# Ninety matmuls of zeros and new planner prices in a gated-linear-attention and expert kernel

## The chip, the core and the metric

The kernel runs on one core of a Trainium2 chip. A core has five engines that run their own queues in order and meet at semaphores: PE (TensorE, the matmuls), DVE (VectorE), ACT (ScalarE), POOL (GpSimd) and SP (SyncE), which here issues all DMA transfers. Matmuls write to PSUM, eight banks; everything else lives in SBUF. DRAM holds inputs and outputs. The metric is device time in microseconds (us), lower is better. The time before is 196.72 us, the median of three runs (196.04 to 197.79).

## The reference

Two steps, one feeding the other. The first is a gated linear attention over 4 batches, 8 heads, 768 positions and a head width of 48; each head keeps a 48 x 48 state that decays per row:

```python
for t in range(S):
    state = alpha[:, :, t, :, None] * state + np.einsum('bhd,bhe->bhde', k[:, :, t], v[:, :, t])
    y[:, :, t] = np.einsum('bhd,bhde->bhe', q[:, :, t], state)
```

The second takes the result as 3072 tokens of width 384 and puts it through a feed-forward layer of 2048 hidden units with a squared ReLU:

```python
h = x @ w_in              # 3072 x 384 @ 384 x 2048
r = np.maximum(h, 0.0)
return (r * r) @ w_out    # 3072 x 2048 @ 2048 x 384
```

All inputs and the output are float32; the kernel multiplies in bfloat16 and sums in float32.

## The kernel before

**Attention.** The 3072 positions are 24 chunks of 128 positions, six to a batch, with all 8 heads of a chunk side by side (384 columns). Within a chunk the recurrence becomes matmuls; from chunk to chunk of a batch only the state goes on. The names used below, with their engine and their line in the profile of before:

- `ln` (ACT, L200): logarithm of alpha. `pm` (PE, L208 and four one-column matmuls L212): running sum of the logarithms, by a triangular matrix `utri`; the last chunk of a batch leaves the one-column matmuls out.
- `ainv`, `am` (ACT, L217, L222): the exponentials of minus and plus that sum. `km` (POOL, L225): k times `ainv`. `qm` (DVE, L228): q times `am`. `vc` (POOL, L204): v cast to `vb`.
- `tr` (PE, L234, eight transposes into the bank `pt`), `qkT` (DVE, L238): both products turned over. From chunk 14 on (`N_PE`) a transposing DMA on SP's queue (L310) does it.
- `sc` (PE, L246): scores. `sm` (DVE, L251): masked scores.
- `av` (PE, L260 and L265, the bank `py`): old state and scores times values; 12 matmuls, or 8 in the first chunk of a batch. `xn` (ACT, L291): result in bfloat16.
- `st` (PE, L274), `dec` (DVE, L282), `sb` (ACT, L286 and L287): state update, decay and a copy.
- `px` (PE, L296), `xT` (DVE, L301): the result turned over, as the feed-forward step needs it; from chunk 14 on by a transposing DMA (L306).

**Feed-forward.** Tokens are taken in nine groups of 2, 2, 3, 3, 3, 3, 3, 3 and 2 chunks. For each group 16 units `ph` (PE, L393, three matmuls each, over 256 or 384 tokens) make the hidden values; `r` (ACT, L398) is the ReLU, `gT` (DVE, L404) its square. Then each chunk of the group has 16 matmuls of 384 columns into `po` (PE, L427; near the end every other chunk uses the bank of `pm`, and the name is `pom`), in four units of four; ACT or DVE empties the bank into `ob` (L441, L443) and SP stores it (L446). Group 0 needs chunks 0 and 1, group 1 needs 2 and 3, group 2 needs 4, 5 and 6.

**Loads.** SP loads four tiles of 192 KB per chunk (`ld_a`, `ld_k`, `ld_q`, `ld_v`, L353), six chunks deep. The eight parts of the two weight matrices (768 KB each, `wst`, L368) stand between chunks: `w_in` after chunk 3, `w_out` after chunk 4; POOL casts each to bfloat16 (L372).

**PSUM.** `ph` has two banks; `po`, `sc`, the transposes' bank and the bank of `pm` and `py` have one buffer each.

**What sets the order.** A planner written in the kernel, `Plan.run`, plays all operations through on its own clock before anything is emitted. Each operation has an engine, a price, a key (a due time; the smallest key among the ready ones goes first), operations it comes after, and a bank it acquires or releases. What the planner starts is emitted in that order, and that is the order on each engine. The planner's clock is no promise: on the chip an engine waits, in order, for what its next instruction needs. A matmul is finished for its users 0.28 us after its price has passed (`HOP`), but PE itself is taken as free once the price has passed. A tile pool gives out its buffers in turn; who takes the buffer anew has to wait until those who used it before are done, and the tile layer puts in the semaphore waits for that.

Of the kernel before, what the change touches and what calls it, by code (L numbers as in the profile page):

```python
# [8 lines left out]
FP32 = mybir.dt.float32  # L9
BF16 = mybir.dt.bfloat16  # L10
# [4 lines left out]
class Plan:  # L15
# [8 lines left out]
        self.cap = dict(capacity)  # L24

    def add(self, eng, cost, key, emit, after=(), behind=(), acquire=None,
            release=None, load=None):
        op = dict(eng=eng, cost=cost, key=(key, len(self.ops)), emit=emit,
                  after=[o for o in after if o is not None],
                  behind=[o for o in behind if o is not None], acquire=acquire,  # L30
                  release=release, load=load, start=None, done=None)
        self.ops.append(op)
        return op

    def run(self):
        ops, cap = self.ops, self.cap
        waiting = {id(o): 0 for o in ops}
        users = {}
        for o in ops:
            uniq = {id(d): d for d in o["after"] + o["behind"]}  # L40
            waiting[id(o)] = len(uniq)
            for d in uniq.values():
                users.setdefault(id(d), []).append(o)
        ready = [(0.0, o) for o in ops if not waiting[id(o)]]
        free = {o["eng"]: 0.0 for o in ops}
        frees = []
        bus = 0.0
        now = 0.0
        order = []
        while len(order) < len(ops):  # L50
            for r in [f for f in frees if f[0] <= now]:
                frees.remove(r)
                cap[r[1]] += 1
            chosen = None
            for t, o in ready:
                if t > now or free[o["eng"]] > now:
                    continue
                if o["acquire"] and cap[o["acquire"]] < 1:
                    continue
                if chosen is None or o["key"] < chosen["key"]:  # L60
                    chosen = o
            if chosen is None:
                later = [max(t, free[o["eng"]]) for t, o in ready] + [f[0] for f in frees]
                now = min(x for x in later if x > now)
                continue
            o = chosen
            ready = [x for x in ready if x[1] is not o]
            o["start"] = now
            free[o["eng"]] = now + o["cost"]
            if o["load"]:  # L70
                bus = max(bus, now + o["cost"]) + o["load"]
                free[o["eng"]] = max(free[o["eng"]], bus - self.QUEUE)
                done = bus + 1.6
            else:
                done = now + o["cost"] + self.HOP.get(o["eng"], 0.1)
            o["done"] = done
            if o["acquire"]:
                cap[o["acquire"]] -= 1
            if o["release"]:
                frees.append((done, o["release"]))  # L80
            order.append(o)
            for u in users.get(id(o), ()):
                waiting[id(u)] -= 1
                if not waiting[id(u)]:
                    ready.append((max([d["done"] for d in u["after"]]
                                      + [d["start"] + d["cost"] for d in u["behind"]]), u))
        self.order = order
        return order
# [3 lines left out]
def kernel(  # L92
# [10 lines left out]
    nc = tc.nc  # L103
    B, H, S, D = q.shape
    HD = H * D
    P = 128
# [6 lines left out]
    DP = 64  # L113
    NS = 4
    NW = 4
    N_PE = 14

    qr = q.rearrange("b h (c p) d -> b c p h d", p=P)
# [26 lines left out]
    groups, n = [], 0  # L145
# [10 lines left out]
    lns = [consts.tile([P, H, DP], BF16, name=f"ln{i}") for i in range(NS)]  # L156
    qks = [consts.tile([P, 2, H, DP], BF16, name=f"qk{i}") for i in range(NS)]
    sbs = [consts.tile([P, NP, 2 * D], BF16, name=f"sb{i}") for i in range(2)]
    xTs = [consts.tile([P, KT, len(cs) * P], BF16, name=f"xT{g}") for g, cs in enumerate(groups)]

    def setup():
        nc.vector.memset(utri, 1.0)
        nc.gpsimd.affine_select(
            out=utri, in_=utri, compare_op=ALU.is_ge, fill=0.0,
            base=0, pattern=[[0, 1], [1, P]], channel_multiplier=-1,
        )
        nc.vector.memset(ones_col, 1.0)
        nc.vector.memset(lns[0], 0.0)
        make_identity(nc, ident)
        for x in lns[1:] + qks[:2]:  # L170
            nc.vector.memset(x, 0.0)
        for x in qks[2:] + sbs:
            nc.gpsimd.memset(x, 0.0)
# [11 lines left out]
    def o(kind, n):  # L185
        return O.get((kind, n))

    def gla(n):
# [119 lines left out]
        def e_qd():  # L308
# [3 lines left out]

        m = n - NW
        add("ln", "ACT", 0.53, e_ln, [o("ld_a", n), o("pm", n - NS)])
        add("vc", "POOL", 0.62, e_vc, [o("ld_v", n), o("av", m), o("st", m)])
        add("pm", "PE", 0.27, e_pm, [o("ln", n), o("av", n - NW + 1)], acquire="m")
        add("ainv", "ACT", 0.49, e_ainv, [o("pm", n), o("km", m)])
        add("am", "ACT", 0.49, e_am,
            [o("pm", n), o("qm", m), o("ainv", n), o("dec", m)], release="m")
        add("km", "POOL", 0.92, e_km, [o("ainv", n), o("ld_k", n), o("st", n - NS), o("tr", n - NS)])  # L320
        add("qm", "DVE", 0.80, e_qm, [o("am", n), o("ld_q", n), o("tr", n - NS)])
        if n < N_PE:
            add("tr", "PE", 0.45, e_tr, [o("km", n), o("qm", n)], acquire="t")
            add("qkT", "DVE", 0.69, e_qkT, [o("tr", n), o("av", m), o("sc", m)], release="t")
# [36 lines left out]
    def load_w(kind, i):  # L361
        n = d_ff // 4 if kind == "wi" else FT // 4
        sl = slice(i * n, (i + 1) * n)
        shape = [P, KT, n] if kind == "wi" else [P, n, d_model]

        def emit():
            x = T[kind, i] = wst.tile(shape, FP32, name="wst", tag="wst")
            nc.sync.dma_start(out=x, in_=w_in_r[:, :, sl] if kind == "wi" else w_out_r[:, sl, :])  # L368

        def cast():  # L370
            dst = w_in_b[:, :, sl] if kind == "wi" else w_out_b[:, sl, :]
            nc.gpsimd.tensor_copy(dst, T[kind, i])  # L372
        ld = plan.add("SP", 0.5, -1e6 + len(loaded), emit,
                      [o("wc", len(weights) - 4)], loaded[-1:], load=2.17)
        loaded.append(ld)
        O["wc", len(weights)] = O["c" + kind, i] = plan.add("POOL", 1.47, -100.0 + len(weights), cast, [ld])
        weights.append(ld)

    group_of = {n: g for g, cs in enumerate(groups) for n in cs}
# [1 line left out]
    def moe(g):  # L381
# [7 lines left out]
        def unit1(f):  # L389
            def e_mm():  # L390
                ph = T["ph", g, f] = ps_h.tile([P, 4 * P], FP32, name="ph")
                for j in range(KT):
                    nc.tensor.matmul(ph[:, 0:tg], lhsT=w_in_b[:, j, f * P:(f + 1) * P],  # L393
                                     rhs=xT[:, j, 0:tg], start=(j == 0), stop=(j == KT - 1))

            def e_relu():
                r = T["r", g, f] = rp.tile([P, 4 * P], BF16, name="r")
                nc.scalar.activation(r[:, 0:tg], T["ph", g, f][:, 0:tg], AF.Relu)  # L398

            def e_sq():  # L400
                if f == 0:
                    T["gT", g] = gp.tile([P, FT, 4 * P], BF16, name="gT")
                r = T["r", g, f]
                nc.vector.tensor_mul(T["gT", g][:, f, 0:tg], r[:, 0:tg], r[:, 0:tg])  # L404
            u = g * FT + f
            key = k0 + span * f / FT
            prev = O.get(("mm1", u - 1))
            mm = O["mm1", u] = plan.add(
                "PE", 0.65 * part, key, e_mm,
                [o("xT", n) for n in cs] + [O["cwi", f // 4]], [prev], acquire="ph")  # L410
            rl = O["relu", u] = plan.add("ACT", 0.13 + 0.41 * part, key - 4 * PACE, e_relu,
                                         [mm, O.get(("sq", u - 4))], [O.get(("relu", u - 1))],
                                         release="ph")
            free = [O.get(("m2", n, 3)) for n in groups[g - 2]] if g >= 2 else []
            O["sq", u] = plan.add("DVE", 0.12 + 0.34 * part, key - 3 * PACE, e_sq,
                                  [rl] + free, [O.get(("sq", u - 1))])

        def unit2(tt, n, qd):
            bank = "m" if g >= len(groups) - 2 and n % 2 else "po"

            def e_mm():
                if qd == 0 and bank == "po":
                    T["po", n] = ps_o.tile([P, d_model], FP32, name="po")
                elif qd == 0:
                    T["po", n] = ps_m.tile([P, d_model], FP32, name="pom", tag="m")
                for kf in range(4 * qd, 4 * qd + 4):
                    nc.tensor.matmul(T["po", n], lhsT=T["gT", g][:, kf, tt * P:(tt + 1) * P],  # L427
                                     rhs=w_out_b[:, kf, :], start=(kf == 0), stop=(kf == FT - 1))
# [34 lines left out]
    for g in range(len(groups)):  # L463
        u1, u2 = moe(g)
        for u in u1 + u2:
            u()

    with tc.manual_schedule():
        setup()
        for x in plan.run():  # L470
            x["emit"]()
# [30 lines left out]
```

## Time and profile before

| | us |
|---|---|
| median of three runs | 196.72 |
| lowest, highest | 196.04, 197.79 |
| the profiled execution, whole | 198.69 |
| its span, first to last instruction | 196.7 |
| PE busy | 174.7 |
| DVE busy | 130.2 |
| ACT busy | 119.7 |
| POOL busy | 50.0 |

The mean granted clock of TensorE is 0.989 of full speed by the record. The profiled execution lies 1.0% above the median of the runs; it is the one from which durations are taken. "Busy" counts a matmul from its start to its modelled end; since matmuls overlap, a group of short ones is busy for less than the sum of its members. The chain that ended last is followed back from the last instruction; its shares by engine are PE 68%, DVE 9%, DMA 7%, SP's queue 6%, ACT 4%. In a timeline a row has start, length, engine, line, operation, tiles and count, and in brackets how long the engine had been idle and who released it.

### The profile page before, as it was taken

The numbers are of one execution on the slowest core, as the hardware profiler recorded it, in microseconds if no ns is written. First come the engines' busy times: TensorE is split into PE (matmuls) and PEld (weight loads), VectorE is DVE, ScalarE is ACT, GpSimd is POOL, SyncE is SP. The second block draws the span as 40 slices with busy tenths as digits, with TensorE's granted clock in tenths as the row PEclk, the third lists the DMA queues.
The fourth block names the chain that finished last, engine by engine and source line by source line (L and its number), as shares of the span: only waits on it lengthen the run. The fifth ranks groups of instructions, "written<-read, shape, count | busy, mean of one in ns | idle before, by whom it ended". The sixth has DMA issues, their size and how long they took to land.

```text
span 196.7 us, 4408 instructions
## 1 busy us (share of the span) xinstructions
PE 174.7 (89%) x1618; PEld 115.0 (58%) x1618; DVE 130.2 (66%) x260; ACT 119.7 (61%) x293; POOL 50.0 (25%) x67
## 2 busy tenths in 40 slices
PE   0466698599999999999999999998999999999992
PEld 0355475366666666766664666565565666567761
DVE  4366677996488889888956785594686763445311
ACT  3354259437536998788866777665776755465400
POOL 6242464660434233331420321111221000000000
PEclk9999999969999999999999999999999999999999
DMA  6999999999989999898999998999985422111012
GB/s 121 187 188 202 355 308 264 382 214 197 191 174 244 185 202 187 153 223 156 227 140 222 224 206 127 194 200 169 190 186 125 106 72 60 40 41 44 36 44 80
DMA packets 121749, 33.77 MB, mean 172 GB/s; under 512 B 115072, under 2 KB 120192, under 8 KB 121728
## 3 DMA queue, kind: packets, MB, share of 16 engines
q1 hardware_dynamic: 121728, 33.50, 85.3%
q8 instruction: 12, 0.20, 0.5%
q14 instruction: 9, 0.07, 0.1%
HBM read 25.17 MB, written 4.72 MB: 152 GB/s over the span
## 4 chain that ended last, share of the span: by engine, by line
PE 68%; DVE 9%; DMA 7%; SPq 6%; ACT 4%; issue 3%; POOL 1%; ACTq 0%; POOLq 0%
PE ph L393 26%; PE po L427 24%; SPq L353 5%; DMA ld_v<-in_v_dram 5%; DVE gT L404 4%; PE pom L427 4%; PE sc L246 3%; PE pt L234 3%; DMA ld_a<-in_alpha_dram 3%; PE py L265 2%; PE py L260 2%; ACT r L398 2%; PE st L274 1%; PE px L296 1%; PE pm L208 1%
## 5 line engine op out<-in xcount | busy, mean ns | idle before, releaser
L398 ACT ACTIVATE r<-ph 128x384 bf16<-128x384 f32 (+1 forms) x144 | 63.8, 455 | 34.6 <-PE ph L393 33.3
L393 PE MATMUL ph<-xT,w_in_b 128*128 128x384 bf16 (+1 forms) x432 | 81.6, 315 | 2.3 <-ACT r L398 1.5
L404 DVE TENSOR_TENSOR gT<-r 128x384 bf16<-128x384 bf16 (+1 forms) x144 | 56.4, 406 | 35.1 <-ACT r L398 32.9
L427 PE MATMUL po<-w_out_b,gT 128*128 128x384 bf16 x336 | 66.5, 328 | 0.5 <-ACT ob L441 0.4
L393 PEld LDWEIGHTS <-w_in_b 128*128 128x128 bf16 x432 | 40.1, 99 | 23.8 <-issue 5.1
L427 PEld LDWEIGHTS <-gT 128*128 128x128 bf16 x384 | 36.0, 98 | 22.1 <-issue 1.3
L225 POOL TENSOR_TENSOR qk<-ld_k,ainv 128x384 bf16<-128x384 f32 x24 | 22.0, 919 | 53.0 <-ACT ainv L217 53.0
L251 DVE TENSOR_TENSOR sm<-sc,utri 128x1024 bf16<-128x1024 f32 x24 | 29.3, 1221 | 4.0 <-PE sc L246 3.8
L204 POOL CAST vb<-ld_v 128x384 bf16<-128x384 f32 x24 | 13.2, 551 | 40.7 <-DMA ld_v<-in_v_dram 33.5
L228 DVE TENSOR_TENSOR qk<-ld_q,am 128x384 bf16<-128x384 f32 x24 | 17.8, 740 | 7.6 <-ACT am L222 7.5
L200 ACT ACTIVATE ln<-ld_a 128x384 bf16<-128x384 f32 x24 | 12.7, 528 | 9.5 <-DMA ld_a<-in_alpha_dram 9.3
L291 ACT CAST xn<-py 128x384 bf16<-128x384 f32 x24 | 11.5, 478 | 8.6 <-PE py L265 8.6
L217 ACT ACTIVATE ainv<-pm 128x384 bf16<-128x384 f32 x24 | 11.7, 489 | 6.3 <-PE pm L212 5.8
L265 PE MATMUL py<-vb,sm 128*128 128x48 bf16 x192 | 12.2, 190 | 3.7 <-DVE sm L251 2.5
L208 PE MATMUL pm<-ln,utri 128*128 128x384 bf16 x24 | 8.4, 352 | 6.5 <-ACT ln L200 5.6
L265 PEld LDWEIGHTS <-sm 128*128 128x128 bf16 x192 | 10.4, 101 | 6.0 <-DVE sm L251 4.5
L282 DVE TENSOR_TENSOR st<-st,am 128x384 f32<-128x384 f32 x20 | 11.2, 561 | 3.3 <-PE st L274 3.1
L234 PE MATMUL pt<-ident,qk 128*128 128x128 bf16 x112 | 10.5, 246 | 2.7 <-POOL qk L225 1.6
L222 ACT ACTIVATE am<-pm 128x388 f32<-128x388 f32 (+1 forms) x24 | 11.9, 495 | 0.0
L246 PE MATMUL sc<-qkT 64*128 64x128 bf16 x192 | 10.6, 236 | 1.0 <-DVE qkT L238 1.0
L441 ACT COPY ob<-po 128x384 f32<-128x384 f32 x12 | 5.8, 482 | 8.5 <-PE po L427 8.4
L260 PE MATMUL py<-sb,qkT 128*128 128x96 bf16 x80 | 10.8, 212 | 0.0
(34 smaller groups left out, 118.2 us busy)
## 6 DMA issues: line engine op xcount, KB each, us to landing
ld_a<-in_alpha_dram SPq DMA_DIRECT2D x24, 192.0 KB, 4.3
ld_k<-in_k_dram SPq DMA_DIRECT2D x24, 192.0 KB, 4.4
ld_q<-in_q_dram SPq DMA_DIRECT2D x24, 192.0 KB, 4.4
ld_v<-in_v_dram SPq DMA_DIRECT2D x24, 192.0 KB, 4.3
out_dram<-ob SPq DMA_DIRECT2D x24, 192.0 KB, 2.5
wst<-in_moe_w_in_dram SPq DMA_DIRECT2D x4, 768.0 KB, 8.5
wst<-in_moe_w_out_dram SPq DMA_DIRECT2D x4, 768.0 KB, 7.4
qkT<-qk SPq DMA_TRANSPOSE x10, 3.7
```

What stands on the lines that cost most here:

```text
L204: nc.gpsimd.tensor_copy(T["vb", n], T["v", n])
L225: nc.gpsimd.tensor_mul(qk[:, 1, :, 0:D], heads(T["k", n]), heads(T["ainv", n]))
L228: nc.vector.tensor_mul(qk[:, 0, :, 0:D], heads(T["q", n]), heads(T["am", n][:, 0:HD]))
L234: nc.tensor.transpose(pt[:, w, p, :], qk[:, w, 2 * p:2 * p + 2, :], ident)
L246: nc.tensor.matmul(sc[:, i, p, :], lhsT=qkT[r, 1, p, :], rhs=qkT[r, 0, p, :], start=True, stop=True)
L251: nc.vector.tensor_mul(sm.rearrange("s i p t -> s (i p) t"), T["sc", n].rearrange("s i p t -> s (i p) t"), utri.to_broadcast([P, H, P]))
L260: nc.tensor.matmul(py[:, 2 * p * D:2 * (p + 1) * D], lhsT=qkT[:, 0, p, :], rhs=sb[:, p, :], start=True, stop=False, skip_group_check=True)
L265: nc.tensor.matmul(py[:, h * D:(h + 1) * D], lhsT=sm[:, i, p, :], rhs=vb[:, h * D:(h + 1) * D], start=first, stop=True, skip_group_check=True)
L393: nc.tensor.matmul(ph[:, 0:tg], lhsT=w_in_b[:, j, f * P:(f + 1) * P], rhs=xT[:, j, 0:tg], start=(j == 0), stop=(j == KT - 1))
L398: nc.scalar.activation(r[:, 0:tg], T["ph", g, f][:, 0:tg], AF.Relu)
L404: nc.vector.tensor_mul(T["gT", g][:, f, 0:tg], r[:, 0:tg], r[:, 0:tg])
L427: nc.tensor.matmul(T["po", n], lhsT=T["gT", g][:, kf, tt * P:(tt + 1) * P], rhs=w_out_b[:, kf, :], start=(kf == 0), stop=(kf == FT - 1))
```

## The change

Three things are added. First, a tile `blank` of 128 x 512 zeros, set by POOL, and ninety PE operations, the blanks, each one matmul of its first 128 columns with all 512, into a fresh tile of the `po` bank. Nothing reads the result. They have the largest keys of all, so the planner takes one whenever PE has nothing else ready on its clock and the `po` bank is free (`needs`; they do not hold the bank). Second, the planner's model grows: it starts at 1.5 us; PE costs 1.9 times the price until 3.4 us after the first operation marked `dense` (`ph` and the blanks); operations marked `port` on DVE and POOL wait for each other's end, as far as prices go; the first load's queue time is shortened by 0.6 us. Third, three prices change. `po` tiles are allocated 512 columns wide, of which 384 are used, so that the blanks can share the pool.

```diff
+    NBLANK = 90
...
-        now = 0.0
+        held = {"DVE": 0.0, "POOL": 0.0}
+        now = 1.5
+        warm = None
...
-                if o["acquire"] and cap[o["acquire"]] < 1:
+                if o["needs"] and cap[o["needs"]] < 1:
...
+            if o["eng"] == "PE":
+                if o["dense"] and warm is None:
+                    warm = now + 3.4
+                if warm is None or now < warm:
+                    o["cost"] *= 1.9
+            if o["port"]:
+                other = "DVE" if o["eng"] == "POOL" else "POOL"
+                o["cost"] += max(0.0, held[other] - now)
+                held[o["eng"]] = now + o["cost"]
             free[o["eng"]] = now + o["cost"]
             if o["load"]:
-                bus = max(bus, now + o["cost"]) + o["load"]
+                bus = max(bus, now + o["cost"] - 0.6 * (bus == 0.0)) + o["load"]
...
+    blank = consts.tile([P, 4 * P], BF16, name="blank")
...
+        nc.gpsimd.memset(blank, 0.0)
...
-        add("vc", "POOL", 0.62, e_vc, [o("ld_v", n), o("av", m), o("st", m)])
+        add("vc", "POOL", 0.50, e_vc, [o("ld_v", n), o("av", m), o("st", m)], port=True)
...
-        add("qm", "DVE", 0.80, e_qm, [o("am", n), o("ld_q", n), o("tr", n - NS)])
+        add("qm", "DVE", 0.55, e_qm, [o("am", n), o("ld_q", n), o("tr", n - NS)], port=True)
...
-                    T["po", n] = ps_o.tile([P, d_model], FP32, name="po")
+                    T["po", n] = ps_o.tile([P, 4 * P], FP32, name="po")[:, 0:d_model]
...
+    def e_blank():
+        nc.tensor.matmul(ps_o.tile([P, 4 * P], FP32, name="po"), lhsT=blank[:, 0:P],
+                         rhs=blank, start=True, stop=True)
+    for i in range(NBLANK):
+        plan.add("PE", 0.214, 1e6 + i, e_blank, needs="po", dense=True)
```

Left out here: `port=True` also on `km`, on the weight casts and on the squares `sq` (the operation that writes `gT`), whose price per 512 columns goes from 0.34 to 0.30, and `dense=True` on `ph`.

More of the change, by code (lines that the diff above doesn't have):

```diff
@@ L26, in add @@
     def add(self, eng, cost, key, emit, after=(), behind=(), acquire=None,
-            release=None, load=None):
+            release=None, load=None, port=False, dense=False, needs=None):
         op = dict(eng=eng, cost=cost, key=(key, len(self.ops)), emit=emit,
@@ L30, in add @@
                   behind=[o for o in behind if o is not None], acquire=acquire,
-                  release=release, load=load, start=None, done=None)
+                  release=release, load=load, port=port, dense=dense, needs=needs or acquire, start=None, done=None)
         self.ops.append(op)
@@ L319, in gla @@
             [o("pm", n), o("qm", m), o("ainv", n), o("dec", m)], release="m")
-        add("km", "POOL", 0.92, e_km, [o("ainv", n), o("ld_k", n), o("st", n - NS), o("tr", n - NS)])
-        add("qm", "DVE", 0.80, e_qm, [o("am", n), o("ld_q", n), o("tr", n - NS)])
+        add("km", "POOL", 0.92, e_km, [o("ainv", n), o("ld_k", n), o("st", n - NS), o("tr", n - NS)], port=True)
+        add("qm", "DVE", 0.55, e_qm, [o("am", n), o("ld_q", n), o("tr", n - NS)], port=True)
         if n < N_PE:
@@ L375, in load_w @@
         loaded.append(ld)
-        O["wc", len(weights)] = O["c" + kind, i] = plan.add("POOL", 1.47, -100.0 + len(weights), cast, [ld])
+        O["wc", len(weights)] = O["c" + kind, i] = plan.add("POOL", 1.47, -100.0 + len(weights), cast, [ld], port=True)
         weights.append(ld)
@@ L409, in unit1 @@
                 "PE", 0.65 * part, key, e_mm,
-                [o("xT", n) for n in cs] + [O["cwi", f // 4]], [prev], acquire="ph")
+                [o("xT", n) for n in cs] + [O["cwi", f // 4]], [prev], acquire="ph",
+                dense=True)
             rl = O["relu", u] = plan.add("ACT", 0.13 + 0.41 * part, key - 4 * PACE, e_relu,
@@ L414, in unit1 @@
             free = [O.get(("m2", n, 3)) for n in groups[g - 2]] if g >= 2 else []
-            O["sq", u] = plan.add("DVE", 0.12 + 0.34 * part, key - 3 * PACE, e_sq,
-                                  [rl] + free, [O.get(("sq", u - 1))])
+            O["sq", u] = plan.add("DVE", 0.12 + 0.30 * part, key - 3 * PACE, e_sq,
+                                  [rl] + free, [O.get(("sq", u - 1))], port=True)
         def unit2(tt, n, qd):
```

## The prediction

> **What bounds the kernel now.** I read the page's engine line first, then busy time by stage, then the order of time.
>
> ```profile
> PE 174.7 (89%) x1618; PEld 115.0 (58%) x1618; DVE 130.2 (66%) x260; ACT 119.7 (61%) x293; POOL 50.0 (25%) x67
> PE   0466698599999999999999999998999999999992
> PEclk9999999969999999999999999999999999999999
> ...
> 0.00:24.71 24.71, 12.54 (x137) 9.44 (x137) 13.77 (x25) 9.98 (x22) 10.71 (x20) 1.00 1.17 211
> 24.71:62.68 37.97, 33.49 (x315) 23.53 (x314) 30.03 (x54) 21.20 (x57) 16.91 (x16) 0.96 1.05 246
> 62.68:196.70 134.02, 128.70 (x1168) 82.03 (x1167) 86.36 (x182) 88.48 (x214) 22.41 (x32) 1.00 0.75 143
> ```
>
> The last three lines are busy time by stretch (length, PE, PEld, DVE, ACT, POOL, granted clock, DMA). The cuts are mine: 24.71 us is the first expert matmul (`ph`), 62.68 us the first of token group 2. Stage C, after 62.68, is PE's: it idles 5.3 us of 134.0, 3.6 of them after its last matmul. So the end is (start of group 2) + about 134 us of PE work, and a change early in PE's order moves the end by what it moves that start. Stage B (24.71 to 62.68) has 4.5 us of PE idle, stage A (before 24.71) 12.2 us. All blank matmuls stand in A and B.
>
> PE's clock is read from matmul lengths and from the granted clock. In the groups by shape of 24 to 29 us a 256-column `ph` has a mean of 396 ns; from 60 us on a 384-column one has 326 ns. Windows of 3.41 us (length, PE busy, granted clock, DMA, GB/s):
>
> ```profile
> 11.58:15.00 3.42, 3.10 (x33) 1.00 1.43 187
> 25.24:28.65 3.41, 3.41 (x28) 1.00 1.13 343
> 35.50:38.90 3.40, 1.74 (x17) 1.00 1.06 379
> 38.90:42.30 3.40, 2.78 (x18) 0.51 1.15 275
> ```
>
> The record shows half clock only from 38.9 to 42.3, but the lengths show it from the start to 28.7 too (three `ph` matmuls in 0.64 us, later in 0.33). PE becomes fast at the end of a full window (28.65) or one 82% busy (42.3), and slow again after one 51% busy (38.9). A window 91% busy (11.58) did not make it fast; two of the operations in it are the transposes `pt` and `px`.
>
> **The change, part by part.**
>
> *Planner prices (port, queue, POOL 0.50, DVE 0.55, start at 1.5).* They emit nothing; they only reorder. From group 2's first `ph` on, PE's order has the same operations, except that `pt` of chunk 8 and `pm` of chunk 9 now stand ahead of it (0.45 + 0.24 = 0.7 us moved out of C). SP's loads keep their order among themselves; only output stores and DMA transposes shift among them, and stage C's PE idle outside the tail, 1.7 us, bounds what that can gain. I take -0.5 us; bounds -1.7 and +1.5, as much again.
>
> *The memset of `blank`, on POOL.* L173's two memsets of 128x1024 took 1.84 us, so half of one is 0.46 us. POOL's memsets ended at 4.44; 4.90 is still ahead of its first product at 5.71. Nothing on the path, but the first blank starts at 1.43 + 0.46 + a start delay of 0.06 = 1.95 us.
>
> *The ninety blanks.* The planner charges 0.214 us each and puts them where its own clock has PE idle. In the changed kernel's built order stage A reads (b = blank, number = chunk):
>
> ```
> 8b pm0 12b tr0 3b pm1 1b sc0 8b av0 1b tr1 st0 3b pm2 px0 sc1 8b av1 2b st1 tr2 2b pm3 3b
> px1 sc2 8b av2 1b tr3 st2 5b px2 sc3 | ph ...
> ```
>
> That is 65 blanks in 14 runs; stage B has the other 25, in 13 runs. PE takes matmuls in order, so a blank that has begun holds what is behind it. What the planner does not count: every blank allocates a new `po` tile in a pool of one buffer, and in the built program each blank's matmul waits on PE's own semaphore for the blank before it. The trace has no such pair, so I bound its period. PE's semaphore comes at a matmul's modelled end, not at the end of its stream:
>
> ```profile
> 46.28 0.81 PE L427 MATMUL po<-w_out_b,gT 128*128 128x384 bf16 x4
> 48.21 0.81 PE L427 MATMUL po<-w_out_b,gT 128*128 128x384 bf16 x4
> 49.06 0.48 ACT L441 COPY ob<-po 128x384 f32<-128x384 f32 x1 [0.21 <-PE po L427]
> ```
>
> Four `po` matmuls stream in 0.65 us (the chain's figure) and are recorded for 0.81; ACT starts 0.04 us after 49.02. One matmul of 384 columns is 0.326 us from start to end, 0.485 at half clock. A blank has 128 columns more: at 0.65/4/384 = 0.42 ns a column 0.05 us, double when cold, so 0.38 warm and 0.59 cold. With the 0.04 us: **0.42 us per serial blank warm, 0.63 cold**. The lower end is the stream alone, 0.42 ns x 512 = 0.216 (0.43 cold); the upper a start 0.06 us after the release, as `pm` after `ln` (4.49 to 4.55): 0.44. I take 0.42, since the recorded end is when others were released. The first blank of a run finds its predecessor done and costs the stream alone.
>
> The Trainium skill ("TensorE: Matmul & The Clock Gate", sections "Back-to-back issue gap" and "Single matmul latency") gives 216 ns for a matmul of 512 columns in a warm stream and 379 ns for one alone; 0.216 and 0.38, as worked out above from rows, agree with both. By the first figure the change comes out 4 us faster, by the second slower, and the built order says that the second applies.
>
> Stage A, with the clock full from about 8.2 us (two windows after the first blank on the same grid): start 1.95; 51 serial blanks x 0.42 = 21.4; 14 firsts x 0.216 = 3.0; real work at warm spacing (4 `pm` x 0.24, 4 `tr` x 0.45, 4 `sc` x 0.33, `av` 0.20 + 2 x 0.37, 3 `st` and 3 `px` x 0.17) = 6.0; ten cold blanks x 0.21 = 2.1. Sum **34.5 us against 24.71: +9.8**. No cover is left: A's idle was 12.2 us, the blanks want 26.5. Warm real work gives back only 5.4 us: at cold spacing it is 4 `tr` x 0.87, 4 `sc` x 0.56, 2 `av` x 0.64 (the chain's figures) and twice the warm price for the rest, 11.4 in all against 6.0. Loads, casts and exponentials are ready earlier than PE in this sum, so no wait is added.
>
> Stage B: 96 `ph` x 0.11 = 10.6; 64 `po` x 0.163 = 10.4; attention (4 `av`, 3 `st`, 5 `tr`, 6 `pm`, 4 `sc`, 4 `px`) 7.4; blanks 12 x 0.42 + 13 x 0.216 = 7.9. Sum 36.3 against 37.97, plus waits s. Before, PE waited 4.5 us here, for DVE and ACT; some of that falls under blanks, and POOL's casts of the weights stretch DVE's products whatever PE does. s is between 0 and 4.5; I take 2. **B: +0.3** (-1.7 to +2.8).
>
> Sum: 9.8 + 0.3 - 0.7 - 0.5 = **+8.9 us**. The profiled execution took 198.69 us for its span of 196.7, so it would give 207.6; it lies 1.0% above the median of the runs, 196.72, from which the forecast is 205.6.
>
> **The clock.** The gain that could pay for this is a warm clock; the whole cold excess is the 5.4 us in A and, in B, the 18 + 6 cold `ph` (24 x 0.11) and 4 cold `po` (4 x 0.16), 3.3 us. It is in the sums above. Whether serial blanks warm the clock is open: a cold one streams 0.43 of 0.63 us, 68%, which lies between the 82% that sufficed and the window at 11.58, where without transposes about 1.4 of 3.42 us streamed (`st` 0.32, `pm` 0.36, `sc` 0.54, pieces of `av` 0.2; 41%) and did not suffice.
>
> The Trainium skill (same page, "PE-mode transpose") says that transposes do not count as busy in the same way, which the window at 11.58 bears out. It also says (table "Why this matters for your kernels") that only gaps of over 3 us cool PE; the window ending at 38.9 cooled it with none above 1.2 us, so the row decides. By the page the blanks keep the clock once warm; by the row a run of them (0.216 of 0.42, 51%) could lose it.
>
> **Rivals.**
> 1. *The blanks do not warm PE in stage A* (the change fails at what it says). 51 x 0.63 + 14 x 0.43 + 11.4 cold work + 1.95 = 51.5, +26.8; B begins cold (+2.0) but finds everything loaded, so s is 0: +0.3; C -0.7 and its whole bound of -1.7: +24.7, **221**. For it: the 41% row. Against: blanks are no transposes and are 68%.
> 2. *Warm late, or lost again in A*: up to half the way to rival 1, +12 to +17, **209 to 214**.
> 3. *Not slower*: the wait on PE's own semaphore is met when the stream ends, so blanks cost 0.216. A: 1.95 + 65 x 0.216 + 6.0 + 2.1 = 24.1 (-0.6); B: 28.4 + 5.4 + 2 = 35.8 (-2.2); with -1.2: -4, **193**; with s at 4.5, 195. It decides below a period of 0.42 - 8.9/63 = 0.28 us. Against it: ACT's start after the recorded end; nothing for it but the planner's 0.214.
>
> **How the numbers follow.** Forecast (serial, warm by 10 us) 0.57, 201 to 210; rival 2, 0.13; rival 1, 0.18 (about 217 to 224); rival 3, 0.09; the rest, 0.03, near no change. The range 201 to 221 leaves out rival 3 and the upper part of rival 1. Within 1% is about what a measurement of this kernel can tell from no change. Faster 0.09, same 0.04, slower 0.87.
>
> **What would show it.** Right: in the longest runs (8 and 12) the blanks start 0.40 to 0.45 us apart once warm; the first `ph` begins at 33 to 36 us; group 2's first `ph` near 72; the stretch from there to the end stays near 133 us. Blanks 0.22 us apart are rival 3, 0.63 apart throughout A rival 1. Wrong in size: if stage B's waits stay at 4.5 us on top of the blanks, or if stage C gains more than 1.7 us from the new order.

## The result and the profile after

The changed kernel takes **208.95 us** (median of 4 runs, 208.79 to 209.61) against 197.25 us before (4 runs, 196.04 to 198.42): a ratio of **1.060**, 95% interval 1.053 to 1.067, 11.7 us slower. The forecast was 205.6 us, the range 201 to 221. Of the 3.3 us between forecast and result, 1.6 are in the spans (+10.5 against +8.9), 0.5 in the median of before (196.72 then, 197.25 now), and the rest comes from the profiled execution of before, which lay above its median while that of after (208.99) does not.

The page of after, engine line, PE's slices, granted clock, and the group of the blanks:

```profile
span 207.2 us, 4583 instructions
PE 197.4 (95%) x1708; PEld 118.6 (57%) x1708; DVE 128.0 (62%) x260; ACT 119.5 (58%) x293; POOL 51.1 (25%) x68
PE   5999999999899999999999999999999999999993
PEclk9999999999999999999999999999999999999999
...
L485 PE MATMUL po<-blank 128*128 128x512 bf16 x90 | 38.4, 426 | 5.5 <-POOL blank L181 2.0
```

PE is now busy 95% of the span, and 38.4 us of that are blanks: the early digits 0466698 of before have been filled to 9 without anything ending earlier. The three stages, cut as before at the first `ph` and at the first `ph` of group 2 (length, PE, PEld, DVE, ACT, POOL, granted clock, DMA share, GB/s):

```profile
0.00:38.51 38.51, 33.71 (x203) 12.41 (x203) 14.06 (x25) 9.86 (x22) 15.62 (x24) 1.00 1.04 213
38.51:77.05 38.54, 37.13 (x356) 24.63 (x353) 28.81 (x57) 22.13 (x60) 13.15 (x14) 1.00 0.83 184
77.05:207.20 130.15, 126.53 (x1160) 81.56 (x1157) 85.15 (x180) 87.56 (x211) 22.36 (x30) 1.00 0.74 142
```

| stage | before | after | change | forecast |
|---|---|---|---|---|
| A, to the first `ph` | 24.71 | 38.51 | +13.8 | +9.8 |
| B, to group 2's first `ph` | 37.97 | 38.54 | +0.6 | +0.3 |
| C, to the end | 134.02 | 130.15 | -3.9 | -1.2 |
| span | 196.7 | 207.2 | +10.5 | +8.9 |

PE's timeline in stage A (start, length, engine, line, operation, count):

```profile
1.96 5.09 PE L485 MATMUL po<-blank 128*128 128x512 bf16 x8 [1.96 <-POOL blank L181]
6.84 0.52 PE L222 MATMUL pm<-ln,utri 128*128 128x384 bf16 x1
...
7.31 7.63 PE L485 MATMUL po<-blank 128*128 128x512 bf16 x12
14.73 1.06 PE L248 MATMUL pt<-ident,qk 128*128 128x128 bf16 x8
15.59 1.49 PE L485 MATMUL po<-blank 128*128 128x512 bf16 x3
...
17.82 3.41 PE L485 MATMUL po<-blank 128*128 128x512 bf16 x8
21.07 0.36 PE L279 MATMUL py<-vb,sm 128*128 128x48 bf16 x8
```

The run of eight blanks at 17.82: 3.41 us = 7 periods + one recorded length of 0.376, so a period is **0.433 us**. The first runs: 7.63 = 11 periods + 0.59, so 0.64 us, the cold figure (clock at half speed). By the lengths the clock was slow until after 15.6 us and full from about 16.3, though the record of the granted clock shows full speed all along. PE waited for nothing else in stage A: its 4.8 us of idle are the start and the short gaps between serial blanks.

### The profile page after: what moved, and what is told of

It reads as the page before. It is cut to its first block, busy times and chain, and to the rows that moved or that the text cites. A ratio compares the mean times of both kernels' runs of the same rounds, so it can differ in the third digit from the quotient of the medians.

```text
span 207.2 us, 4583 instructions
## 1 busy us (share of the span) xinstructions
PE 197.4 (95%) x1708; PEld 118.6 (57%) x1708; DVE 128.0 (62%) x260; ACT 119.5 (58%) x293; POOL 51.1 (25%) x68
## 4 chain that ended last, share of the span: by engine, by line
PE 92%; DVE 4%; issue 2%; ACT 1%; POOL 0%; POOLq 0%; ACTq 0%
PE ph L407 29%; PE po L442 26%; PE po L485 16%; PE sc L260 4%; PE pom L442 4%; PE pt L248 3%; PE py L279 2%; PE pm L222 2%; DVE gT L418 2%; PE st L288 2%; PE py L274 2%; PE px L310 1%; DVE qk L242 1%; PE pm L226 1%; DVE sm L265 1%
## 5 line engine op out<-in xcount | busy, mean ns | idle before, releaser
L407 PE MATMUL ph<-xT,w_in_b 128*128 128x384 bf16 (+1 forms) x432 | 78.0, 308 | 0.5 <-ACT r L412 0.3
L418 DVE TENSOR_TENSOR gT<-r 128x384 bf16<-128x384 bf16 (+1 forms) x144 | 55.1, 397 | 32.5 <-ACT r L412 30.2
L485 PE MATMUL po<-blank 128*128 128x512 bf16 x90 | 38.4, 426 | 5.5 <-POOL blank L181 2.0
L242 DVE TENSOR_TENSOR qk<-ld_q,am 128x384 bf16<-128x384 f32 x24 | 16.9, 707 | 6.3 <-ACT am L236 5.5
L485 PEld LDWEIGHTS <-blank 128*128 128x128 bf16 x90 | 8.1, 100 | 20.0 <-issue 17.5
L252 DVE COPY qkT<-pt 128x1024 bf16<-128x1024 bf16 x14 | 9.6, 685 | 12.4 <-PE pt L248 12.4
L279 PE MATMUL py<-vb,sm 128*128 128x48 bf16 x192 | 11.2, 183 | 0.2 <-DVE sm L265 0.2
L279 PEld LDWEIGHTS <-sm 128*128 128x128 bf16 x192 | 9.7, 96 | 2.3 <-DVE sm L265 0.4
L274 PE MATMUL py<-sb,qkT 128*128 128x96 bf16 x80 | 9.8, 204 | 0.0
L260 PE MATMUL sc<-qkT 64*128 64x128 bf16 x192 | 9.5, 219 | 0.0
```

Of the source, the lines that this page charges most:

```text
L242: nc.vector.tensor_mul(qk[:, 0, :, 0:D], heads(T["q", n]), heads(T["am", n][:, 0:HD]))
L260: nc.tensor.matmul(sc[:, i, p, :], lhsT=qkT[r, 1, p, :], rhs=qkT[r, 0, p, :], start=True, stop=True)
L274: nc.tensor.matmul(py[:, 2 * p * D:2 * (p + 1) * D], lhsT=qkT[:, 0, p, :], rhs=sb[:, p, :], start=True, stop=False, skip_group_check=True)
L279: nc.tensor.matmul(py[:, h * D:(h + 1) * D], lhsT=sm[:, i, p, :], rhs=vb[:, h * D:(h + 1) * D], start=first, stop=True, skip_group_check=True)
L485: nc.tensor.matmul(ps_o.tile([P, 4 * P], FP32, name="po"), lhsT=blank[:, 0:P], rhs=blank, start=True, stop=True)
```

## The experiments

Times of the first `ph`, of group 2's first `ph` and the span are from the profiled executions; ratios are against the kernel before, run on the same chip. For e3, e4 and e7 there is a single time and no interval.

| run | first ph | group 2 | span | time | ratio (95%) |
|---|---|---|---|---|---|
| before | 24.71 | 62.68 | 196.7 | 197.25 | |
| after | 38.51 | 77.05 | 207.2 | 208.95 | 1.060 (1.053 to 1.067) |
| e1 no blank emitted | 24.16 | 62.23 | 197.1 | 198.75 | 1.005 (1.003 to 1.008) |
| e2 blanks not serial | 24.67 | 62.70 | 198.7 | 200.36 | 1.012 (1.008 to 1.017) |
| e3 ones | 39.24 | 77.78 | 210.4 | 212.21 | |
| e4 old planner | 44.68 | 84.88 | 219.4 | 221.46 | |
| e5 blanks of A only | 39.46 | 77.06 | 210.5 | 210.35 | 1.064 (1.056 to 1.071) |
| e6 blanks of B only | 24.04 | 63.65 | 197.5 | 199.23 | 1.005 (1.002 to 1.008) |
| e7 narrow blanks | 28.53 | 63.51 | 197.7 | 199.49 | |
| e8 before + 48 blanks | 24.80 | 59.61 | 196.8 | 198.99 | 1.006 (1.002 to 1.010) |
| e9 stores on ACT | 39.34 | 77.88 | 207.9 | 209.31 | 1.058 (1.052 to 1.064) |
| e10 before, 8 buffers | 24.86 | 60.58 | 196.0 | 197.68 | 0.999 (0.996 to 1.002) |
| e11 e8, 8 buffers | 24.58 | 60.74 | 197.8 | 199.55 | 1.008 (1.004 to 1.012) |
| e12 e8, less to load | 23.91 | 59.27 | 191.6 | 194.22 | 0.985 (0.977 to 0.992) |

### e1: the same order, no blank emitted

```diff
     def e_blank():
-        nc.tensor.matmul(ps_o.tile([P, 4 * P], FP32, name="po"), lhsT=blank[:, 0:P],
-                         rhs=blank, start=True, stop=True)
+        pass
```

> The planner still plans the ninety blanks, so every real operation keeps the order of the changed kernel, but no blank matmul is emitted. If the loss is the time that the blanks hold PE (my theory), all of it goes: first ph near 24.7 us as before, and the time falls to 192 to 197 us. Where in that interval tells where stage C's 3.9 us came from: near 193 if the new order made stage C shorter (then it stays near 130 us), near 196 if it was shorter only because loads had got ahead of a late PE (then it returns to about 133 us). If the new order itself makes the kernel slow (rival), the time stays near 209 us.

Measured: 198.75 us, ratio 1.005, above the 192 to 197 expected. The new order by itself costs 0.5%, about 1 us; the other 5.5% are the blanks. Stage C is 134.9 us here, so C's 3.9 us in the changed kernel do not come from the order alone.

### e2: all blanks, but none waits on the one before

```diff
     def e_blank():
-        nc.tensor.matmul(ps_o.tile([P, 4 * P], FP32, name="po"), lhsT=blank[:, 0:P],
-                         rhs=blank, start=True, stop=True)
+        if T.get("blank") is None:
+            T["blank"] = ps_o.tile([P, 4 * P], FP32, name="po")
+        nc.tensor.matmul(T["blank"], lhsT=blank[:, 0:P], rhs=blank, start=True, stop=True)
...
                 if qd == 0 and bank == "po":
+                    T["blank"] = None
```

> All ninety blanks, same order, but consecutive blanks share one tile of the po bank, so that none waits on the one before it. If the wait on PE's own semaphore is the cost (my theory), blanks follow each other 0.43 us apart cold and 0.216 us warm, PE is warm by about 8 us, the first ph begins at 24 to 26 us, and the time is 190 to 196 us. If it is PE's latency for each blank whatever the wait, they stay 0.43 to 0.64 us apart and the time near 209 us.

Measured: 200.36 us, ratio 1.012. PE's timeline of e2:

```profile
1.95 3.59 PE L488 MATMUL po<-blank 128*128 128x512 bf16 x8 [1.95 <-POOL blank L181]
5.81 3.03 PE L488 MATMUL po<-blank 128*128 128x512 bf16 x12
8.68 0.61 PE L248 MATMUL pt<-ident,qk 128*128 128x128 bf16 x8
```

Twelve blanks from 5.81 to 8.68: 2.87 us is one cold one (0.43) and eleven warm ones (0.216), so the clock was full from about 6.4 us and the pipelined price is as expected. The first `ph` is back at 24.67 us. So the wait on PE's own semaphore is what stage A paid for. But the time is not 190 to 196 us: with PE warm from 6.4 us and the blanks out of the way, group 2 still begins at 62.70 us, as it does in e1 with a slow clock until about 27 us. In stage B, PE waits in both for POOL's casts of `w_out` (total, times, longest; e1, then e2):

```profile
PE po L442 <- POOL w_out_b L386: 3.2, 3, 1.7
PE po L443 <- POOL w_out_b L386: 1.9, 3, 0.7
```

**The warm clock gained nothing.**

### e3: ones in place of zeros

```diff
-        nc.gpsimd.memset(blank, 0.0)
+        nc.gpsimd.memset(blank, 1.0)
```

> The blank tile holds ones in place of zeros; order and waits are those of the changed kernel. If the blanks' streaming share of 0.43 in 0.64 us is what left the clock slow until about 15.6 us, nothing changes: cold until 14 to 17 us, first ph near 38.5 us, time near 209 us. If zeros do not count as activity, the clock is full by about 8 us, some ten blanks and the first transposes cost half, and the first ph comes 2.5 to 4 us earlier, time 205 to 206.5 us.

Measured: the eight and twelve blanks take 5.09 and 7.63 us, as with zeros; the clock rises near 17.9 us, not earlier; first `ph` at 39.24. Zeros are not the reason for the slow clock. The single time of 212.2 us lies 3 us above the expected 209; in its profile `sc` waits 2.0 us for a transposing DMA in stage C, which it does not in the profile of after. Whether that comes with the ones or from run to run, a single run cannot tell.

### e4: the blanks under the old planner

All new prices, the start at 1.5, the warm factor and the port rule taken out again; the ninety serial blanks stay (76 ahead of the first `ph`). The lines of the prices are left out here.

```diff
-        now = 1.5
+        now = 0.0
...
-            if o["eng"] == "PE":
-                if o["dense"] and warm is None:
-                    warm = now + 3.4
-                if warm is None or now < warm:
-                    o["cost"] *= 1.9
-            if o["port"]:
-                other = "DVE" if o["eng"] == "POOL" else "POOL"
-                o["cost"] += max(0.0, held[other] - now)
-                held[o["eng"]] = now + o["cost"]
```

> The ninety serial blanks with the planner's old clock and prices (start at 0, no warm factor, no port, old prices). Its order has 76 blanks before the first ph in place of 65. By my theory stage A is 43 to 45 us, stage B some 3.5 us shorter than with the change; the time is 210 to 215 us, nearer 211 if stage C is near 130 us without the new order (loads ahead), nearer 214 if it is back at 133 us or more (the new order made it short). If the new prices cause the loss (rival), the time is near 197 us.

Measured: 221.46 us. Stage A is 44.7 us, as the blanks' price says; B is 40.2 and not shorter (PE waits 2.8 us for one `qkT`, and the clock falls once), C 134.5. The new prices are not the cause of the loss: with the old ones the blanks cost more. The time expected was too low by 6 us, all of it in B and C. Group 2 starts at 84.88 us, later than in the changed kernel, and still C is not near 130 us: a late start alone does not make it so, at least in this single run.

### e5 and e6: which blanks cost

```diff
     def e_blank():
+        T["nb"] = T.get("nb", 0) + 1
+        if T["nb"] > 65:    # e5; e6: <= 65
+            return
```

> The changed kernel's order and serial blanks, but only the 65 blanks ahead of the first ph are emitted; the 25 of stage B are left out. If the whole loss is PE's time in stage A (theory), the first ph stays at 38.5 us, stage B gives back at most its 8 us of blanks, and the time is 202 to 208 us. If the blanks of stage B do the harm (rival), the time falls to about 199 us.

> Only the 25 blanks from the first ph on are emitted. First ph near 24.2 us as without blanks. Stage B had some 5 us of PE idle without them and they want 8 to 8.6 us: if they fall into the idle time, the time stays near 199 us; if they stand in front of what DVE and ACT wait for, it is up to 203 us.

Measured: e5 1.064, e6 1.005. The 65 blanks of A are the whole loss; the 25 of B, left alone, cost no time beside e1 (B is 1.5 us longer, C 1.0 us shorter). But e5 lies above the 202 to 208 us expected and did not come down by B's 8 us: without any blank, stage B still took 37.6 us, and C 133.4. Stage B of e5, five microseconds in it (length, PE, PEld, DVE, ACT, POOL, granted clock, DMA share, GB/s), and a product of DVE just before:

```profile
39.46:77.06 37.60, 33.03 (x330) 22.85 (x327) 29.27 (x56) 21.82 (x60) 13.13 (x14) 0.95 0.84 186
50.00:55.00 5.00, 3.90 (x23) 2.48 (x24) 5.00 (x9) 1.43 (x4) 3.44 (x3) 0.77 1.04 188
48.84 1.81 DVE L242 TENSOR_TENSOR qk<-ld_q,am 128x384 bf16<-128x384 f32 x1
```

PE idles 4.6 us there. For 2.0 of them it waits for this product, which takes 1.81 us beside the casts of `w_out` (0.55 in chunks 1 to 3 of before, with no weight cast beside it), and afterwards the clock falls. Before, the same stood in stage B: the product took 1.85 us beside the casts, PE waited 1.2 us for it, and the clock fell to 0.51. POOL's timeline of after shows that the casts moved along with PE:

```profile
30.65 0.91 POOL L239 TENSOR_TENSOR qk<-ld_k,ainv 128x384 bf16<-128x384 f32 x1 [5.03 <-issue]
31.51 0.50 POOL L218 CAST vb<-ld_v 128x384 bf16<-128x384 f32 x1
31.95 6.02 POOL L386 CAST w_in_b<-wst 128x1536 bf16<-128x1536 f32 x4
46.28 0.91 POOL L239 TENSOR_TENSOR qk<-ld_k,ainv 128x384 bf16<-128x384 f32 x1 [8.30 <-ACT ainv L231]
47.13 0.58 POOL L218 CAST vb<-ld_v 128x384 bf16<-128x384 f32 x1
47.66 6.20 POOL L386 CAST w_out_b<-wst 128x1536 bf16<-128x1536 f32 x4
```

The casts of `w_in` stand in POOL's queue behind the product `km` of chunk 3, which waits for `pm` of chunk 3, which stands behind the blanks on PE. They ran at 22.57 to 30.5 us before and run at 31.95 to 38 now. The first of them frees a `wst` buffer, so `w_out` is fetched from 33.4 us instead of 29.6, and its casts stand behind chunk 4's `km`: they began at 34.9 before and begin at 47.7 now. Stage B thus moved as a whole, its supplies with it.

### e7: narrow blanks

```diff
-        nc.tensor.matmul(ps_o.tile([P, 4 * P], FP32, name="po"), lhsT=blank[:, 0:P],
-                         rhs=blank, start=True, stop=True)
+        nc.tensor.matmul(ps_o.tile([P, 4 * P], FP32, name="po")[:, 0:P], lhsT=blank[:, 0:P],
+                         rhs=blank[:, 0:P], start=True, stop=True)
```

> All ninety serial blanks, each 128 columns wide in place of 512. If the wait for the blank before sets the price (theory), a blank still costs 0.27 us warm and 0.32 cold, five times its stream; the first ph begins at 28 to 31 us and the time is 200 to 204 us. If the stream were the price, it would be 0.05 to 0.11 us, the first ph at 24 to 25 us and the time near 199 us. Streaming a third of the time, these blanks should leave the clock slow in all of stage A if the streaming share is what counts.

PE's timeline of e7, a cold and a warm run:

```profile
5.00 3.79 PE L485 MATMUL po<-blank 128*128 128x128 bf16 x12
22.61 2.16 PE L485 MATMUL po<-blank 128*128 128x128 bf16 x8
```

From start to start these are 0.32 us cold and 0.27 warm, as expected: a quarter of the stream, but half the price when cold and over six tenths when warm. A 128-column matmul streams in 0.107 us cold and 0.056 warm (starts of the transposes in after and e2), so the wait adds 0.21 to 0.22 us to the stream at either width and either clock (0.64 less 0.43, 0.433 less 0.216, 0.32 less 0.107, 0.27 less 0.056). The first `ph` comes at 28.53 us, as expected, but the time is only 199.5 us, in one run: of 4.4 us lost in stage A against e1, 3.1 us came back in B (35.0 us). A slip of 4 us in A is absorbed, one of 14 us is not. By the lengths of the blanks the clock rose near 17.8 us in spite of the small streaming share, and it fell again near 24.5:

```profile
17.60:24.50 6.90, 5.93 (x62) 3.43 (x62) 4.95 (x7) 3.02 (x8) 3.06 (x5) 1.00 1.06 316
24.50:28.00 3.50, 3.25 (x33) 2.53 (x33) 2.36 (x3) 0.79 (x2) 3.50 (x3) 0.51 1.08 371
```

PE is busy 86% of the first stretch, with no gap above 0.06 us. So neither the share of streaming of the blanks alone nor the longest gap says when the clock changes.

### e8: the order of before, with blanks that do not wait

Planner and order of before; 8 blanks ahead of everything, 10 behind `pm` of chunk 0, 3 behind each of the first four `tr`, 6 behind each of the first three `sc`. Left out here: the tile `blank`, its memset on POOL and the 512 columns of `po`, as in the change.

```diff
-        for x in plan.run():
-            x["emit"]()
+        zero = ps_o.tile([P, 4 * P], FP32, name="po")
+        def blanks(k):
+            for _ in range(k):
+                nc.tensor.matmul(zero, lhsT=blank[:, 0:P], rhs=blank, start=True, stop=True)
+        behind = {id(O["pm", 0]): 10}
+        for n in range(4):
+            behind[id(O["tr", n])] = 3
+        for n in range(3):
+            behind[id(O["sc", n])] = 6
+        blanks(8)
+        for x in plan.run():
+            x["emit"]()
+            blanks(behind.get(id(x), 0))
```

> The kernel before with its own order and planner, plus 48 blanks that share one tile and so do not wait on each other, written in at fixed places of stage A where PE idled. PE is warm from about 8 us. If the slow clock of the first 29 us was worth something (what would speak for blanks as such), the time falls by 2 to 3 us to about 195 us. If the first ph waits for w_in and stage B for w_out, whatever the clock (theory), first ph stays at 24.1 to 24.7 us, group 2 begins at 61.5 to 62.7 us, and the time is within 1% of before.

PE's timeline of e8:

```profile
24.80 2.10 PE L395 MATMUL ph<-xT,w_in_b 128*128 128x256 bf16 x12 [1.54 <-POOL w_in_b L374]
59.61 1.14 PE L395 MATMUL ph<-xT,w_in_b 128*128 128x384 bf16 x6
```

PE is early in stage A and then stands 1.54 us for the cast of `w_in`. Group 2 begins 3 us earlier than before, outside what was expected (up to 2 us of that need not come from the blanks: e10, the order of before without any but with eight load buffers, has 60.58); yet the time is 1.006 of before, not less, because stage C takes 137.2 us. So an early start of group 2 is worth nothing here, and a clock warm from the start neither.

### e9: does the load stream or PE hold the end?

In the changed kernel SP stood behind the first output store, with the loads of chunk 8 behind it:

```profile
51.01 0.68 SPq L367 DMA_DIRECT2D ld_a<-in_alpha_dram  x1
60.91 0.36 SPq L461 DMA_DIRECT2D out_dram<-ob  x1
61.33 0.43 SPq L367 DMA_DIRECT2D ld_k<-in_k_dram  x1
61.84 0.65 SPq L367 DMA_DIRECT2D ld_q<-in_q_dram  x1
```

```diff
-                    nc.sync.dma_start(out=out_r[n], in_=T["ob", n])
+                    q = nc.scalar if n < 4 else nc.sync
+                    q.dma_start(out=out_r[n], in_=T["ob", n])
```

> The changed kernel, with its first four output stores issued by ACT in place of SP, so that SP does not stand for 9 us (51.7 to 60.9) behind the first store with the loads of chunk 8 and later behind it. If the late load stream sets the end (theory L), ld_a of chunk 8 is issued near 55 us in place of 63.2 and the time falls by 3 to 8 us, to 201 to 206. If PE's late start sets it (theory P: group 2 begins at 77 us and stage C is already at PE's floor of 130 us), the stream moves and the time stays at 208 to 210 us.

Measured: `ld_a` of chunk 8 is issued at 55.20 us, 8 us earlier, and the time is 209.31 us, ratio 1.058: no change. But the lead does not last: chunk 15 is 1.8 us earlier than in after, chunk 18 0.3, and the last chunk comes at 149.28 against 148.93. The end of the stream did not move, so this run alone does not decide between the two. PE's row of stage C does:

```profile
77.88:207.90 130.02, 126.46 (x1160) 81.54 (x1157) 84.70 (x180) 87.50 (x211) 22.21 (x30) 1.00 0.69 132
```

PE idles 3.6 us of 130.0, all of them after its last matmul, as in after. In the changed kernel PE holds the end.

### e10, e11 and e12: what holds the end when PE is early

```diff
-    NLD = 6
+    NLD = 8
```

> The kernel before with eight load buffers per tensor in place of six; PE's order is the same. If in stage C the loads wait for free buffers, the stream of the later chunks runs ahead, PE's idle and stretched time there (134.0 against the 130.2 seen with a lead) goes in part, and the time falls by 1 to 3 us. If the stream is held by the transfers themselves, no change within 0.5%.

> Eight load buffers and the 48 piped blanks on the order of before. There group 2 began 3 us earlier (59.6 us) and stage C took 3 us longer. If late loads ate the gain, deeper buffers give it back: 194 to 196 us, the best version. If the stream is held by the transfers themselves, the time stays at 198 to 199 us.

e12, on top of e8, leaves out the load of q from chunk 7 on:

```diff
+                if name == "q" and n >= 7:
+                    T["q", n] = T["k", n]
+                    return
                 x = T[name, n] = loads.tile([P, HD], FP32, name="ld_" + name)
```

> The kernel of e8 (order of before, 48 piped blanks, group 2 from 59.6 us), but from chunk 7 on q is not loaded and k stands in for it, so that the result is not the reference's; 17 of 96 load transfers fall away, PE's work is the same. If the load stream is what keeps the end at 196 to 198 us when PE starts group 2 early (theory), the issue times of ld_a move forward by about 1 us per chunk, stage C shrinks from 137 towards PE's floor of 130 us and the time falls to 191 to 196 us. If PE's own work or another wait holds the end, the stream moves and the time stays within 1% of 199 us.

Issue times of `ld_a` on SP's queue, for chunk 8 and the last chunk, from the timelines:

```
             chunk 8   chunk 23     span
before        53.38     139.22      196.7
e1            52.02     138.64      197.1
e2            52.34     140.63      198.7
e8            53.43     138.52      196.8
e10           52.34     138.43      196.0
e12           52.51     130.38      191.6
after         63.17     148.93      207.2
e9            55.20     149.28      207.9
```

Deeper buffers changed nothing (e10 0.999; e11 1.008, beside 1.006 for e8) and did not move the stream forward by more than 1.6 us: waiting for buffers is not what holds the loads. With a quarter of the later loads gone the stream's end moves from 138.5 to 130.4 us and the time falls to 194.2 us, with the same PE work and group 2 at the same place. The ratio is 0.985 against 1.006 for e8, some 4 us (the two ran on different chips); against before that is not clearly more or less than 2%, but its interval (0.977 to 0.992) and that of e8 do not meet. So **with PE in time, the transfers hold the end** of this kernel. Stage C of e8 and of e12 (length, then PE busy), and how long ACT's `ln` waited for `ld_a` in stage C up to 150 us, in before and in e8:

```profile
59.61:196.80 137.19, 129.88 (x1168) 82.08 (x1167) 86.55 (x182) 88.20 (x214) 23.23 (x32) 1.00 0.81 144
59.27:191.60 132.33, 127.96 (x1168) 82.08 (x1167) 86.96 (x182) 89.02 (x214) 23.90 (x32) 1.00 0.63 124
ACT ln L200 <- DMA ld_a<-in_alpha_dram: 5.3, 4, 2.0
ACT ln L202 <- DMA ld_a<-in_alpha_dram: 10.2, 10, 1.8
```

PE idles 7.3 us in C of e8 and 4.4 in that of e12, of which 3.6 and 3.9 come after its last matmul; in C of after it idles 3.6, all after the last. In e12, as in after and e9, `ln` does not wait for `ld_a` at all. Whether it is the transfers' rate or their order on SP's queue that holds the stream was not separated. No version tried beats the kernel before while it does all of its work.

## Why the prediction was right, and where it was not

Right: the sign, the range, the mechanism that loses the time, and its price. Of the signs named beforehand the period of the blanks came (0.433 us, within 0.40 to 0.45); the first `ph` at 38.51 us (33 to 36), group 2 at 77.05 (near 72) and the stretch after it of 130.2 us (near 133) did not. That the time still lies within the 201 to 210 us of the forecast is partly luck, as below.

- *Serial blanks.* "Each blank's matmul waits on PE's own semaphore" was priced at 0.42 us warm and 0.63 cold; measured 0.433 and 0.64. e2 takes the wait away and the 13.8 us of stage A are gone; e7 narrows the stream to a quarter and the price falls only by half (cold) or a little under four tenths (warm).
- *Stage A, +9.8, was +13.8.* The step that failed in size is "with the clock full from about 8.2 us" and its term of ten cold blanks: 20 blanks and the first transposes were cold, and the clock rose during the next run. From the timeline the 14 runs take 29.5 us (26.5 with the cold term, as forecast) and the real work 7.0 us (6.0). Of the 4 us, 2.2 are cold blanks, 0.6 cold `pm` and `tr`, 0.7 the period (51 x 0.013), 0.3 the three `px` (0.26 us each, not 0.17), the rest is spread over the other operations.
- *"Loads, casts and exponentials are ready earlier than PE"* held for stage A, where PE waited for none, but not for what A hands on: the casts stand in POOL's queue behind a product that waits for PE, so they moved by 9 and 13 us.
- *Stage B, +0.3, was +0.6*, and much as summed: the blanks took PE's time and its waits shrank under them, from 3.9 us to 0.5. Not foreseen was that without these blanks B is nearly as long (e5, 37.6 us), because it moves as a whole, casts, stretched products and slow clock with it.
- *Planner prices, -0.5 and 0.7 moved out of C.* e1, with the order alone, is about 1 us slower than before, where the two terms together had -1.2 (-2.4 to +0.8); its C is 134.9 us, not shorter.
- *"A change early in PE's order moves the end by what it moves that start"* is the step of the reading that failed. It holds only for a late start. Group 2 began between 59.6 and 63.7 us in eight kernels with all loads (before, e1, e2, e6, e7, e8, e10, e11), and their spans lie between 196.0 and 198.7 us in no order. Stage C has two limits: PE's 130 us from group 2's start, and the load stream. Before, the second held, with 134.0 us; a start 14.4 us late left the stream ahead and C at PE's floor, so 3.9 us came back where I had 1.2. This error and that in A have opposite signs and hid each other. Nor does every late start give 130 us: in e3, e5 and e4 group 2 begins at 77 to 85 us and C takes 132.6, 133.4 and 134.6, and `ln` waits 3.7, 2.8 and 3.7 us for `ld_a`, in after and e9 not at all. How far the new order helps the late start there stays open (e3 and e4 are single runs, and the profiled execution of e5 is the slowest of its four).
- *Rival 3 (not slower, 193 us)* fell twice. The wait does serialize. And where it is taken away (e2), the sum of that rival is wrong too: it counted PE time saved in B, which was never on the path.
- *Rival 2 (warm late)* is what happened in stage A: the clock was full at about 16 us, not by 10 as the forecast's branch has it. The time, 208.95 us, lies just under the 209 where that rival began, because C gave back more than reckoned.
- *Rival 1 (cold through stage A)* was half right: the serial blanks did not warm PE for 12.8 us, then the clock rose in the run of blanks behind the first dense transposes. The Trainium skill ("TensorE: Matmul & The Clock Gate", Part 1) gives a warm-up budget of about 3.4 us of time, however many matmuls; the pipelined blanks of e2 were warm after about 4.4 us, the serial ones of after, e3 and e5 not after 12.8 and those of e4 not after 19. The rule on gaps that the prediction cited fits after, where the clock, once full, was kept through the serial runs, but not e7, which lost it with no gap above 0.06 us, nor e5, which lost it after a wait of 2.0 us.
- *The clock as the gain that could pay.* The 5.4 and 3.3 us of cold excess were real lengths, but worth nothing in time (e2, e8).

The extra 0.5% of the new order without blanks (e1) was not taken apart by a run. In its stage C, `sc` waits 2.3 us for transposing DMAs, in that of before not at all.

## What to carry to other kernels

A filler instruction is free only if nothing real stands behind it when it runs, in its own queue or in the queues that wait on that one; an in-order engine makes it a promise about time that a planner's clock cannot keep. Before matmuls are added to warm PE, look whether PE's slow stretch is on the path at all, and whether each new tile puts a wait between consecutive fillers. A stage in which an engine is busy 96% may still be held by transfers: take a part of the loads away and see whether the end moves.

## What the runs showed of the hardware

- Two matmuls of 512 columns that meet only through PE's own semaphore follow each other after 0.433 us (0.64 cold), against 0.216 (0.43) in a stream; for 128 columns it is 0.27 and 0.32 us, against 0.056 and 0.107 in a stream. That is the recorded length of one plus about 0.05 us, or the stream plus 0.21 to 0.22 us in all four cases.
- A serial chain of such matmuls, recorded as busy for 91% of the time, left the clock at half speed for 12.8 us (after) and 19 us (e4); filled with ones it did the same (e3). A dense stream had it full after about 4.4 us (e2). What share of what activity counts was not settled: with narrow serial blanks, streaming a third of the time, the clock was full near 17.8 us (e7).
- The clock fell to half near 24.5 us in e7 although PE had no gap above 0.06 us in the 6.9 us before; in after it stayed full through serial runs of 512 columns.
- In the slow stretches at the start of after, e3, e4 and e7 the record of the granted clock shows full speed and only the matmul lengths show the half; the later fall in e7 is in the record (0.51).
